# Mirrored rows by gather and scatter, one more DMA transpose, and second norms on ScalarE in a fused convolution and FFN kernel

## The chip, the cores and the metric

The kernel runs on one core of a Trainium2 chip. The metric is the device time of one execution in microseconds; lower is better. The engines are TensorE (PE), VectorE (DVE), ScalarE (ACT), GpSimd (POOL) and SyncE (SP), which here only issues DMAs.

## The reference

The input is a sequence of 2048 rows of 640 channels, in bf16. A long convolution per channel, done by FFT over 4096 points, is followed by a gated feed-forward network; both have a layer norm before them and a residual.

```python
def _A_ref(q, k, v, shift_k, ssm_k, ssm_D):        # q is the normed x
    k_shift = sum(k_pad[:, t:t + S, :] * shift_k[:, 3 - t] for t in range(4))
    kv = k_shift * v
    y = irfft(rfft(pad(kv)) * rfft(pad(ssm_k)))[:S]    # per channel, then bf16
    return q * (y + kv * ssm_D)
def _B_ref(x, w_gate, w_up, w_down):               # 640 -> 1728 -> 640
    return (silu(x @ w_gate) * (x @ w_up)) @ w_down
h  = x + _A_ref(layernorm(x), A_k, A_v, A_shift_k, A_ssm_k, A_ssm_D)
h2 = h + _B_ref(layernorm(h), B_w_gate, B_w_up, B_w_down)
```

(Cut and condensed from the original; `x` is `A_q`.)

## The kernel before

The 2048 rows are four blocks of 512, each of four tiles `q` of 128 rows. The convolution is done by block: each block of `kv` is transformed by matmuls with a fixed cosine and sine basis (`x_transform`, matrix `WX`), each segment of 512 taps of the filter likewise (`g_transform`, matrix `WG`). The spectra are multiplied and added by block pairs on DVE (`pair`, line 444, operations on 128x2560 elements), and the sums go back by `inverse` (matrix `WI`, line 598). `hbuild` joins the spectra of neighbouring segments.

The transforms use symmetry: the rows of tiles 0 and 1 of a block are needed in mirrored order. For `kv` PE mirrors them with a flip matrix (`front`, line 419; for block 0 the shift itself is made by matmuls with shifted identity matrices, `front_first`, line 394). In `inverse`, even and odd parts `es` and `os` give, by sum, tiles 2 and 3 in natural order and, by difference, tiles 1 and 0 in mirrored order. With `HOW[n] == "J"` PE flips that difference back (group `"J"`, line 618: 4 matmuls of 320 columns for each of two halves of a block), and DVE multiplies it out of PSUM (line 621).

The filter segment `p` is needed with taps on partitions. `gload` either loads it plainly and turns it with 20 matmuls of 128 columns and four ACT copies (lines 315 and 319), or, where `TRANS` names the segment, uses one DMA transpose of 640 KB issued by SP (line 304). The skip weight `ssm_D` (`drow`) is added to tap 0 of segment 0 by five one-row matmuls (line 317).

A layer norm has statistics (`ln`; on ACT lines 528 to 532, or on DVE for block 0's second norm), a power -1/2 on POOL (`root`, line 551), and a scaling (`scale`), on DVE (line 564) or ACT (lines 560 and 561). `XACT` lists the pairs (block, norm) with the scaling on ACT. Before each pow a small DVE reduction is placed, the "port op" (`port`, line 538): [...] the pow waits for it. For pairs in `XACT` a one-element DVE copy of `rstd` (line 553), called the `h` copy below, follows the pow.

The normed rows `hl` go through a DMA transpose to `hT` (line 649), and `ffn` runs gate and up projections (line 686, 512 columns), evicts them on ACT (lines 691 and 698), multiplies on DVE (line 700), and does the down projection (line 717, 320 columns). For blocks 0 to 2 the residual is added on PE (line 714) and ACT copies the result out (line 723); for block 3 DVE adds it (line 725). Output tiles use two buffers `ot`, by `m % 2`.

PSUM has four tiles: two ("A") for the convolution, two ("F") for filter transforms and FFN; a group takes one until its eviction.

The order is written out: every step is registered with `add(engine, ...)` and numbered, and `SEQUENCE` is a list of all 1017 numbers. Each engine runs its steps in that order, SP and POOL their DMA issues too, and waits where data aren't there. The list came from a planner, for which `pr`, `t0`, `lag`, `kb` and the durations are costs; they have no effect once the list is written out.

`HOW`, `BACK`: with `HOW[n] == "G"` a block's first two tiles of `x` are gathered from HBM in mirrored order (`load_x`, `mirror`, two indirect DMAs on POOL, by a table of indices `idx`), the difference needs no flip, and its residual is added mirrored; with `BACK[n] == "S"` output tiles 0 and 1 are scattered back by indirect DMAs on POOL, each after a port op that waits for the output copy.

Of the kernel before, what the change touches and what calls it, by code (L numbers as in the profile page):

```python
# [16 lines left out]
D = 640  # L17
FF = 1728
P = 128
# [74 lines left out]
ACC = ()  # L94
MOVES = ()
RES = (0, 1, 2)
XACT = [(n, 1) for n in (1, 2, 3)]
VEC = (0,)
SPAN = 96
TURN = ()  # L100
HOW = 'JJJJ'
BACK = "SSSS"
TRANS = {2: 28, 3: 28}
WARM = (0.43, 5, 0)
SEQUENCE = [int(i) for i in """
0 19 205 5 1 8 67 3 7 20 6 21 77 23 4 2 10 11 76 13 12 14 15 17 16 68 18 70 69 71 72 62 74 73 22 75 59 32 51 56 52 49 63 57 78 54 79 50 64 80 26 53 81
24 55 84 25 27 28 58 204 85 30 213 60 29 31 82 33 61 212 83 90 41 65 34 86 88 87 66 35 42 206 9 92 100 89 207 43 93 101 122 208 94 44 118 102 91 95 45
333 103 96 214 46 104 97 47 36 105 98 215 48 106 99 216 37 107 217 110 226 154 38 227 39 209 155 109 221 234 196 40 220 332 108 162 320 197 170 163
111 164 171 112 188 113 134 189 114 228 135 165 116 115 222 172 117 229 156 173 119 223 123 157 230 136 120 124 190 231 121 445 142 158 446 191 125
138 137 126 198 159 127 143 199 160 235 144 192 161 128 139 224 210 140 193 178 145 211 141 225 200 179 146 129 437 321 218 201 180 147 219 194 132  # L110
181 130 133 148 232 166 195 149 233 131 182 167 186 260 183 252 439 174 253 261 152 168 249 175 153 237 262 184 169 150 447 151 263 254 202 187 438
255 185 256 203 448 264 176 247 265 257 266 177 246 322 236 323 440 267 250 324 258 325 327 239 248 328 240 344 449 339 329 345 326 251 330 340 331
334 441 341 450 259 269 335 342 356 336 346 343 337 357 268 238 351 338 270 347 353 368 460 348 352 459 349 442 272 454 363 354 241 350 364 355 242
271 408 358 369 407 243 273 359 360 380 405 276 361 274 365 375 366 244 275 370 367 376 392 362 377 461 381 277 278 393 284 434 371 279 378 285 281
280 394 435 382 404 372 406 373 453 300 286 374 383 301 282 379 306 462 298 302 283 482 387 384 385 388 299 287 386 389 463 307 390 433 395 290 291
396 308 391 397 443 309 400 398 455 288 415 573 289 464 436 678 416 312 677 561 401 399 417 292 402 303 313 293 304 409 403 305 456 310 418 296 311
457 410 297 294 479 419 411 295 444 480 412 451 413 421 314 452 483 414 420 422 458 423 315 465 670 318 427 316 319 466 485 424 317 493 501 481 574
428 502 562 425 487 429 494 430 484 495 467 568 669 496 488 431 503 497 486 504 563 498 491 505 565 585 564 489 569 566 506 499 567 468 586 679 575
570 571 576 671 500 577 580 578 572 490 581 582 597 469 579 587 598 509 426 583 588 472 680 507 584 592 492 508 589 593 590 609 511 470 604 610 594
591 595 510 605 599 596 513 606 600 471 621 512 539 607 622 474 517 608 601 515 475 616 514 602 617 473 603 611 516 618 518 612 633 540 672 634 613  # L120
519 476 635 614 673 477 674 541 712 520 619 526 521 522 628 681 525 615 682 629 542 620 692 523 630 691 527 623 631 432 524 547 624 528 632 625 544
641 711 626 531 636 642 627 713 643 548 813 532 637 801 693 685 529 686 645 530 714 646 543 644 647 638 533 549 534 639 545 675 550 651 640 553 546
535 554 648 537 694 652 538 649 687 551 653 536 552 478 695 654 715 802 663 676 650 814 555 688 683 664 684 556 689 655 696 665 690 656 559 557 560
666 697 657 717 558 658 716 667 659 698 660 719 741 661 699 733 742 808 718 734 743 810 720 809 735 721 811 803 744 702 812 804 825 723 805 662 820
806 826 722 700 815 701 807 816 724 837 817 821 818 725 822 832 823 838 668 736 819 824 827 703 727 737 849 706 833 726 738 829 828 728 745 830 850
739 729 834 839 835 740 831 840 836 841 731 704 844 842 730 746 845 861 846 856 749 847 862 705 857 848 843 707 732 747 851 748 708 858 751 852 874
859 873 853 863 860 854 875 245 709 750 868 753 864 909 869 855 754 865 757 866 761 752 779 765 870 876 710 755 871 780 877 758 756 881 922 872 759
867 882 883 781 760 878 762 766 879 763 891 782 764 783 884 767 892 769 880 768 770 893 784 785 771 894 773 786 788 772 775 885 776 787 774 886 910
791 789 792 887 777 790 778 895 888 795 793 903 797 921 794 896 798 904 889 796 905 799 800 906 897 907 890 898 899 900 916 901 917 918 911 919 920
912 913 933 923 914 934 915 924 925 928 926 927 929 930 945 940 931 946 932 941 942 935 943 944 936 937 957 947 938 958 939 948 949 952 950 951 953  # L130
954 969 908 959 955 970 956 964 965 966 982 981 961 960 902 967 976 962 983 963 977 968 978 971 979 972 973 984 974 975 985 980 986 989 987 988 993
990 991 994 992 995 999 996 1000 997 1001 1002 1011 1003 1012 1004 998 1013 1014 1005 1015 1006 1016 1007 1008 1009 1010
""".split()]


def dve(n, psum=False):
    return (120 + n) / 960 if psum else 0.06 + n / 1920
# [7 lines left out]
def kernel(  # L145
# [123 lines left out]
    def load(q, dst, src, w, pr, kb, r=(), dur=0.45, after=(), t0=0.0):  # L269
        eng = {"SP": nc.sync, "ACT": nc.scalar, "POOL": nc.gpsimd}[q]  # L270
        before = plan.stage
        if not before and w:
            plan.stage = "load " + w[0]
        add(q, dur, lambda: eng.dma_start(out=dst, in_=src), r=r, w=w, pr=pr, kb=kb, after=after, t0=t0)
        plan.stage = before
# [25 lines left out]
    @stage  # L301
    def gload(p, pr, q="SP"):
        if p in TRANS:
            add("SP", 5.5, lambda: nc.sync.dma_start_transpose(gT[p], A_ssm_k[:, p * MB:(p + 1) * MB]), w=[f"gT{p}"], pr=pr, kb=640, t0=TRANS[p])
            return
        kc = kch[p % 2]
        load(q, kc, A_ssm_k[:, p * MB:(p + 1) * MB].rearrange("(c q) t -> q c t", q=P), [f"kch{p % 2}"], pr, 760)
        for kt in range(4):
            g = (TP[p], "T", p, kt)

            def mm(g=g, kt=kt):
                out = ps(g).rearrange("p a b -> p (a b)")
                for c in range(5):
                    dd = p == 0 and kt == 0
                    nc.tensor.matmul(out[:, c * P:(c + 1) * P], kc[:, c, kt * P:(kt + 1) * P], ident, start=True, stop=not dd)
                    if dd:
                        nc.tensor.matmul(out[:, c * P:(c + 1) * P], ident[0:1, :], drow[:, c * P:(c + 1) * P], start=False, stop=True)
            add("PE", 0.6, mm, r=["flip", f"kch{p % 2}"] + (["drow"] if p == 0 and kt == 0 else []), w=[g], pr=pr + 50, acq=(TP[p], g))
            add("ACT", act(D), lambda g=g, kt=kt: nc.scalar.copy(gT[p][:, kt, :], ps(g).rearrange("p a b -> p (a b)")[:, 0:D]),
                r=[g], w=[gTk[p]], pr=pr - 40, rel=(TP[p], g))  # L320

    def wcast(t):
        g = ("A", "w", t)
# [49 lines left out]
        return bass.AP(tensor=kk.tensor, offset=kk.offset + row * D, ap=[[D, n], [1, 4 * D]]).rearrange("p (a b) -> p a b", a=4)  # L373

    def first_loads():
        load("SP", kfirst[:], kk[0:MB, :].rearrange("(m p) d -> p m d", p=P), ["x1_0", "x1_1", "x1_2", "x1_3"], -98, 640)
        load("SP", hT[0][:].rearrange("p a b -> p (a b)").rearrange("p (a b) -> p a b", a=4), vv[0:MB, :].rearrange("(m p) d -> p m d", p=P), ["v0all"], -96, 640)
        load("SP", WG, WG_h.ap(), ["WG0", "WG1"], -95, 1024)

    @stage  # L380
# [281 lines left out]
    def ffn(n, pr):  # L662
# [38 lines left out]
        if n == 0:  # L701
            down_loads()
        plan.stage = f"down {n}"
        for m in range(4):
            gr = ("F", "D", n, m)
            back = m < 2 and HOW[n] != "J" and BACK[n] == "T"
            out_by = "S" if m < 2 and HOW[n] != "J" and BACK[n] == "S" else ""
            res = n in RES or back
            parts = [(0, 4), (4, 8), (8, 12), (12, 14)]
            for i, (c0, c1) in enumerate(parts):  # L710
                def mm(gr=gr, m=m, c0=c0, c1=c1, res=res, back=back):
                    if c0 == 0 and res:
# [6 lines left out]
                add("PE", 2 * (c1 - c0 + (i == 0 and res)) * 0.137, mm, r=[f"wd{i}"] + (["wd4", "tz", "wz"] if i == 3 else []) + [f"x{b}_{m}", (("F", "U", n, 13), 0)] + [f"tT{c}" for c in range(c0, c1)] + ([(gr, i - 1)] if i else []),  # L719
                    w=[(gr, i)], pr=pr + 20 + m, acq=("F", gr) if i == 0 else None)  # L720
            s = m % 2
            if res:
                add("ACT", act(D), lambda gr=gr, m=m, s=s: nc.scalar.copy(r3(ot[s][:]), ps(gr)[:, :, 0:NH]), r=[(gr, 3)], w=[f"o{s}"], pr=pr - 9000, rel=("F", gr))
            else:
                add("DVE", dve(D, True), lambda gr=gr, m=m, s=s: TA(r3(ot[s][:]), ps(gr)[:, :, 0:NH], r3(xin[b][:, m, :])), r=[(gr, 3), f"x{b}_{m}"], w=[f"o{s}"], pr=pr - 9000, rel=("F", gr))
# [90 lines left out]
```

## Time and profile before

| what | us |
|---|---|
| median of 3 runs | 289.55 (289.06 to 289.61) |
| profiled execution, its own time | 288.89 |
| its span, first to last instruction | 287.1 |
| PE busy | 277.1 |
| DVE busy | 220.8 |
| ACT busy | 198.4 |
| POOL busy | 18.6 |
| HBM traffic over the span | 139 GB/s |

The profile is of one execution. "Busy" of PE includes matmuls that overlap in the pipeline, so counts times the spacing of back-to-back matmuls say more than the share. The chain of waits is followed back from the last instruction, and names for each piece the engine and line that held it. A group's row reads: line, engine, operation, output and inputs, shapes, count, busy time and mean nanoseconds, then idle time before it and who ended it. In the DMA rows, "us to landing" is from issue until the data are there.

### The profile page before, as it was taken

The page shows a single profiled execution, that of the slowest core. Times are in us where ns is not written, and L with a number is a line of the kernel's source. Part 1 is how long each engine was busy: PE and PEld are TensorE (multiplying, and loading weights), DVE is VectorE, ACT ScalarE, POOL GpSimd, SP SyncE. Part 2 cuts the span into 40 slices and gives each one's busy share as a digit, 9 for nine tenths or more (in the row PEclk, how much of TensorE's full clock was granted, in tenths as well). Part 3 has the DMA queues.
Part 4 walks back from the last instruction along what each step waited for, and adds up shares of the span by engine and source line. Part 5 has one row for each costly group of instructions (what it writes and reads, how often), then busy time and mean ns, then how long its engine had stood idle before and what let it go on. Part 6 is the DMA issues. An engine that isn't in the chain of part 4 may idle for free.

```text
span 287.1 us, 4448 instructions
## 1 busy us (share of the span) xinstructions
PE 277.1 (97%) x1680; PEld 164.3 (57%) x1680; DVE 220.8 (77%) x299; ACT 198.4 (69%) x388; POOL 18.6 (6%) x22
## 2 busy tenths in 40 slices
PE   7899999999999999999999999999999989999994
PEld 2577777776444546764455467645455665444673
DVE  1738999999999999999999999999997511111222
ACT  5898755878785999367879995498958954545300
POOL 0003000010001001300004011000100110000000
PEclk9999999999999999999999999999999999999999
DMA  7999691363369847685653567456441391665011
GB/s 222 327 289 257 171 354 32 116 183 71 87 172 313 232 169 199 141 221 173 161 138 69 177 191 184 116 160 159 99 109 46 32 200 24 159 158 143 1 48 46
DMA packets 67946, 44.13 MB, mean 154 GB/s; under 512 B 25490, under 2 KB 66003, under 8 KB 67796
## 3 DMA queue, kind: packets, MB, share of 16 engines
q1 hardware_dynamic: 67778, 43.64, 56.0%
q8 instruction: 13, 0.21, 0.3%
q10 hardware_dynamic: 146, 0.20, 0.3%
q14 instruction: 9, 0.07, 0.1%
HBM read 37.28 MB, written 2.62 MB: 139 GB/s over the span
## 4 chain that ended last, share of the span: by engine, by line
DVE 54%; PE 22%; ACT 10%; DMA 7%; issue 5%; SPq 0%; DVEq 0%; ACTq 0%
DVE s L444 19%; DVE T L444 13%; PE psF L686 10%; PE psF L717 8%; DVE k L362 5%; DVE tT L700 3%; DMA hT<-in_A_v_dram 3%; PE psA L394 2%; DMA wu<-in_B_w_up_dram 2%; DMA k<-in_A_k_dram 2%; DVE k L367 2%; ACT sg L691 2%; ACT xln L561 2%; ACT junk L531 2%; ACT uc L698 2%
## 5 line engine op out<-in xcount | busy, mean ns | idle before, releaser
L686 PE MATMUL psF<-hT,wg 128*128 128x512 bf16 x280 | 68.6, 379 | 0.7 <-ACT uc L698 0.7
L686 PE MATMUL psF<-hT,wu 128*128 128x512 bf16 x260 | 63.6, 379 | 0.2 <-DMA wu<-in_B_w_up_dram 0.2
L717 PE MATMUL psF<-wd,tT 128*128 128x320 bf16 x448 | 63.3, 299 | 0.0
L717 PEld LDWEIGHTS <-tT 128*128 128x128 bf16 x448 | 43.8, 98 | 17.2
L444 DVE TENSOR_TENSOR s<-s,T 128x2560 bf16<-128x2560 bf16 x32 | 47.4, 1493 | 0.1
L444 DVE TENSOR_TENSOR T<-s,s 128x2560 bf16<-128x2560 bf16 x32 | 47.3, 1491 | 0.0
L691 ACT ACTIVATE sg<-psF 128x512 bf16<-128x512 f32 (+1 forms) x56 | 33.2, 596 | 20.2 <-DVE tT L700 12.0
L700 DVE TENSOR_TENSOR tT<-sg,uc 128x512 bf16<-128x512 bf16 (+1 forms) x56 | 23.0, 424 | 30.7 <-ACT uc L698 30.4
L686 PEld LDWEIGHTS <-wg 128*128 128x128 bf16 x280 | 27.4, 98 | 31.1 <-issue 1.2
L686 PEld LDWEIGHTS <-wu 128*128 128x128 bf16 x260 | 25.3, 98 | 30.2 <-DMA wu<-in_B_w_up_dram 0.7
L698 ACT CAST uc<-psF 128x512 bf16<-128x512 f32 (+1 forms) x56 | 32.8, 586 | 10.3 <-PE psF L686 9.8
L551 POOL TENSOR_TENSOR rstd<-var,mhalf 128x2 f32<-128x2 f32 (+2 forms) x15 | 18.1, 1207 | 213.9 <-ACT var L532 181.2
L345 PEld LDWEIGHTS <-s 128*128 128x128 bf16 x256 | 25.0, 98 | 9.7
L347 ACT CAST s<-psF 128x640 bf16<-128x640 f32 x32 | 22.1, 696 | 11.2 <-PE psF L345 11.1
L345 PE MATMUL psF<-wd,s 128*128 128x320 bf16 x192 | 28.5, 299 | 0.0
L439 ACT CAST s<-psA 128x640 bf16<-128x640 f32 x29 | 19.5, 696 | 9.4 <-PE psA L434 9.4
L531 ACT ACTIVATE junk<-x,sm 128x640 uint8<-128x640 bf16 x28 | 23.2, 830 | 0.5
L434 PE MATMUL psA<-kv,WX 128*128 128x320 bf16 x128 | 21.0, 299 | 0.0
L444 DVE TENSOR_TENSOR s<-s,s 128x2560 bf16<-128x2560 bf16 x14 | 20.8, 1487 | 0.0
L528 ACT ACTIVATE junk<-x 128x640 uint8<-128x640 bf16 x28 | 20.7, 738 | 0.0
L598 PE MATMUL psA<-s,WI 128*128 128x320 bf16 x128 | 19.0, 299 | 0.3 <-DVE s L444 0.2
L362 DVE TENSOR_TENSOR k<-k,w 128x2560 bf16<-128x2560 bf16 x12 | 17.7, 1488 | 0.0
(72 smaller groups left out, 242.9 us busy)
## 6 DMA issues: line engine op xcount, KB each, us to landing
k<-in_A_k_dram SPq DMA_DIRECT2D x12, 640.0 KB, 5.5
wu<-in_B_w_up_dram SPq DMA_DIRECT2D x24, 320.0 KB, 3.8
wg<-in_B_w_gate_dram SPq DMA_DIRECT2D x24, 320.0 KB, 3.3
x<-in_A_q_dram SPq DMA_DIRECT2D x4, 640.0 KB, 7.4
out_dram<-o SPq DMA_DIRECT2D x16, 160.0 KB, 2.1
v<-in_A_v_dram SPq DMA_DIRECT2D x12, 160.0 KB, 3.2
wd<-in_B_w_down_dram SPq DMA_DIRECT2D x3, 640.0 KB, 6.4
tT<-in_A_ssm_k_dram SPq DMA_DIRECT2D x2, 640.0 KB, 7.8
```

Of the source, the lines that this page charges most:

```text
L345: nc.tensor.matmul(ps(g)[:, h, 0:NH], WG[:, kt, ct * P:(ct + 1) * P], gT[p][:, kt, h * NH:(h + 1) * NH], start=(kt == 0), stop=(kt == 3))
L347: add("ACT", act(D), lambda g=g, ct=ct: nc.scalar.copy(r3(G[p][ct // 4][:, ct % 4, :]), ps(g)[:, :, 0:NH]), r=[g], w=[Gk[p] + "cs"[ct // 4 ...
L362: add("DVE", dve(4 * D), lambda: nc.vector.tensor_mul(kd[:], kd[:], w4[:]), r=["w4"] + ks, w=[kn], pr=pr)
L434: nc.tensor.matmul(ps(g)[:, h, 0:NH], WX[:, kt, ct * P:(ct + 1) * P], kv[:, base + kt, h * NH:(h + 1) * NH], start=(kt == 0), stop=(kt == 1))
L444: add("DVE", dve(n * D), lambda: f(o, a, b), r=ks(ak) + ks(bk), w=ks(ok), after=["WG0", "WG1"] if ok[:2] == "s7" else [], pr=pr)
L528: add("ACT", 0.74, lambda: nc.scalar.activation(junks[j][:], src, ACT.Copy, scale=-1.0 / D, accum_out=s[:, 0:1]), r=[xk], w=[k + "a", f"ju ...
L531: nc.scalar.activation(junks[j][:], src, ACT.Square, bias=s[:, 0:1], accum_out=s[:, 1:2])
L686: i = nc.tensor.matmul(ps(gr)[:, which, :], w[:, kt, cc * P:(cc + 1) * P], hT[b][:, kt, :], start=(kt == 0), stop=(kt == 4))
L691: apart(gr, 0, nc.scalar.activation(sg[s][:z, :], ps(gr)[:z, 0, :], ACT.Silu))
L698: add("ACT", act(MB), lambda gr=gr, s=s, z=z, merged=merged: nc.scalar.copy(uc[s][:z, :], ps(gr)[64:128, 0, :] if merged else ps(gr)[:, 1, ...
L700: add("DVE", dve(MB), lambda c=c, s=s, z=z: TM(tT[:z, c * MB:(c + 1) * MB], sg[s][:z, :], uc[s][:z, :]), r=[f"sg{s}", f"uc{s}"], w=[f"tT{c ...
L717: nc.tensor.matmul(ps(gr)[:, h, 0:NH], tT[:, c * MB + m * P:c * MB + (m + 1) * P], wd[:, c, h * NH:(h + 1) * NH], start=(c == 0 and not re ...
```

## The change

- `TRANS` names segment 1 too, so `gload(1)` is one DMA transpose on SP in place of a plain load, 20 matmuls and four ACT copies.
- `HOW` is `"GGJJ"`: blocks 0 and 1 gather tiles 0 and 1 of `x` mirrored (four indirect DMAs on POOL), their `inverse` has no `"J"` matmuls, and output tiles 0 and 1 of both blocks are scattered (four indirect DMAs on POOL, each with a port op before it). SP loads the index table `idx` first.
- `XACT` gains (0, 1), (1, 2) and (2, 2): four scalings of block 0's first norm and eight of the second norms of blocks 1 and 2 move from DVE to ACT; each of these roots gets an `h` copy on DVE.
- `drow` is added to tap 0 of segment 0 by one DVE operation on one partition instead of five matmuls.
- The last output tile is done half by half: 14 matmuls for columns 0 to 319, their addition and store, then the other half.
- `SEQUENCE` is new. SP now starts with `idx`, `drow`, segment 0, `k` and `v` of block 0, `WX`, the transpose of segment 1, tiles 2 and 3 of `x`, `WG`; before, it started with a `v` tile of block 1, segment 1, `k`, `v`, `x`, segment 0, `drow`, the transpose of segment 2, `WG`, `WX`. The transposes of segments 2 and 3 now follow each other after `WI`. PE turns segment 0 first, then does the shifts of tiles 2, 0, 1, 3 and then three groups of `g_transform(0)` before `x_transform(0)`; before, segment 1 came first, and the turning of segment 0 stood between shifts 3, 0, 1, 2. On POOL the gathers of block 0 come first; each gather of block 1 stands before a root; the first scatter of block 0 stands before the root of block 1's tiles 3 and 0, the second after it; both scatters of block 1 stand after block 2's last root. On ACT the new second-norm scalings stand beside the output copies of the down projections of blocks 0 and 1. The new `h` copies stand far behind their roots.

```diff
-XACT = [(n, 1) for n in (1, 2, 3)]
+XACT = [(n, 1) for n in range(4)] + [(1, 2), (2, 2)]
...
-HOW = 'JJJJ'
+HOW = 'GGJJ'
 BACK = "SSSS"
-TRANS = {2: 28, 3: 28}
+TRANS = {1: 0, 2: 0, 3: 0}
 WARM = (0.43, 5, 0)
 SEQUENCE = [int(i) for i in """
...
             def mm(g=g, kt=kt):
                 out = ps(g).rearrange("p a b -> p (a b)")
                 for c in range(5):
-                    dd = p == 0 and kt == 0
-                    nc.tensor.matmul(out[:, c * P:(c + 1) * P], kc[:, c, kt * P:(kt + 1) * P], ident, start=True, stop=not dd)
-                    if dd:
-                        nc.tensor.matmul(out[:, c * P:(c + 1) * P], ident[0:1, :], drow[:, c * P:(c + 1) * P], start=False, stop=True)
+                    nc.tensor.matmul(out[:, c * P:(c + 1) * P], kc[:, c, kt * P:(kt + 1) * P], ident, start=True, stop=True)
...
+        if p == 0:
+            add("DVE", dve(D), lambda: TA(gT[0][0:1, 0, :], gT[0][0:1, 0, :], drow), r=["drow"], w=[gTk[0]], pr=pr - 40)
...
+        def last_tile(gr, m, s):
+
+            def done(h, i):
+                if not h:
+                    apart(gr, 0, i)
+
+            for h in range(2):
+                cols = slice(h * NH, (h + 1) * NH)
+
+                def mm(h=h, cols=cols):
+                    for c in range(14):
+                        i = nc.tensor.matmul(ps(gr)[:, h, 0:NH], tT[:, c * MB + m * P:c * MB + (m + 1) * P], wd[:, c, cols], start=(c == 0), stop=(c == 13))
+                        if h:
+                            apart(gr, 1, i)
...
+                add("DVE", (120 + NH) / 960, lambda h=h, cols=cols: done(h, TA(ot[s][:, cols], ps(gr)[:, h, 0:NH], xin[b][:, m, cols])),
+                    r=[(gr, h), f"x{b}_{m}"], w=[f"o{s}h{h}"], after=[f"o{s}"], pr=pr - 9000, rel=("F", gr) if h else None)
+                load("SP", oo[n * MB + m * P:n * MB + (m + 1) * P, cols], ot[s][:, cols], [], pr - 300, 80, r=[f"o{s}h{h}"])
...
+            if (n, m) == (NB - 1, 3):
+                last_tile(gr, m, s)
+                continue
```

## The prediction

> **What bounds the kernel now.** I read the totals first, then three stretches of the span, then the chain that ended last, and then the queues at the start. Totals and stretches (columns: stretch, its length, and each engine's busy time with its instructions):
>
> ```profile
> PE 277.1 (97%) x1680; PEld 164.3 (57%) x1680; DVE 220.8 (77%) x299; ACT 198.4 (69%) x388; POOL 18.6 (6%) x22
> 0.00:21.90 21.90, 18.85 (x113) 11.21 (x114) 9.24 (x11) 16.51 (x32) 0.47 (x7) 1.00 0.94 280
> 21.90:253.00 231.10, 227.80 (x1388) 135.32 (x1385) 205.01 (x276) 172.70 (x342) 18.11 (x15) 1.00 0.58 154
> 268.30:283.60 15.30, 15.20 (x112) 10.72 (x110) 3.00 (x6) 1.17 (x2) 0.00 (x0) 1.00 0.10 33
> ```
>
> A busy PE is not a PE at its peak, so I count work. In the chain
>
> ```profile
> 253.00 15.28 PE psF L686 x70
> 268.29 15.23 PE psF L717 x112
> 283.54 0.82 DVE o L725
> ```
>
> nothing stands between matmuls: a 512-column one costs 15.28/70 = 0.218 us, a 320-column one 15.23/112 = 0.136 us. The first spectral transform of block 0 (line 345) starts at 21.90. From there to 283.5 PE has 540 of the first (117.6 us) and 1028 of the second (139.8 us): 257.4 us of work in 261.6. So only 4.2 us is lost after 21.9. PE's work bounds the kernel, with the late start and a 3.6 us tail around it. DVE, 205 of 231 us busy in the long stretch, runs close behind: it must feed PE on time.
>
> The start, as three engines show it:
>
> ```profile
> 6.60 1.25 PE L315 MATMUL psF<-perm,tT 128*128 128x128 bf16 x10
> 11.47 3.26 PE L394 MATMUL psA<-s,perm 128*128 128x320 bf16 x14
> 21.90 3.42 PE L345 MATMUL psF<-wd,s 128*128 128x320 bf16 x24
> 25.16 1.25 PE L434 MATMUL psA<-kv,WX 128*128 128x320 bf16 x8
> ...
> 6.27 7.90 SPq L304 DMA_TRANSPOSE wd<-in_A_ssm_k_dram  x1
> 14.21 0.58 SPq L274 DMA_DIRECT2D s<-const_wg  x1
> 22.46 5.43 SPq L304 DMA_TRANSPOSE hT<-in_A_ssm_k_dram  x1
> ```
>
> PE turns filter segment 1, waits for `v`, does shifts between the turns of segment 0 and reaches line 345 only at 21.90; the input transform (line 434) waits for DVE until 25.16. A transpose of 640 KB holds SP for 5.4 to 7.9 us, and what follows waits.
>
> **The change, part by part.**
>
> *PE.* Two inverses lose their J matmuls: 16 of 32 on line 618, 16 x 0.136 = -2.2 us, all in the full stretch. Twenty turning matmuls of segment 1 and five for `drow` go too, from the start, where they count only through the start time.
>
> *Start.* Segment 0 is now loaded first, then `k`, `v`, `WX`, then the transpose of segment 1. The first product waited for `k` (issued 1.66, product at 8.70). Now 640 KB lies ahead of it instead of 800, with issue some 0.4 us later: I take 8.4. Products of tiles 2, 1, 0 end at 8.4 + 3 x 1.44 = 12.7. PE: `v` still near 10.4, its turn to 11.5, tile 2's shift 3.26 to 14.8, `v`'s second turn 0.6, tile 0 to 16.4, tile 1 (14 x 0.149) to 18.4, tile 3 to 20.4. So line 345 starts near 20.3, not 21.90: -1.6 us. Tile 3's product with `v` (0.82) and the two sums (0.8 each) follow to 22.9, so line 434 starts at 22.9, 2.2 earlier; the three G groups put ahead of it (3 x 1.09) cover the gap. The new addition of `drow` (nearest row, 0.49 us) lies while DVE waits for a shift. `WG` now stands behind 2.4 MB, the transpose and half of `x`. [...] the traced transposes took 5.4 and 7.9 us for 640 KB; [...] by the trace SP is free at 12.5 and `WG` (5.7 us before) lands at 18 to 19. [...] both are ahead of 20.3, the second barely. If it is 3 us worse, the gain is gone. Bounds: +1.5 to -3. The transposes of segments 2 and 3 move to after 20 us; their users come 16 groups later (past 35), cover enough.
>
> *DVE.* Twelve scalings leave for ACT (4 for block 0's first norm, 8 for the second norms): 12 x 0.44 = -5.3. Each half of two inverses trades 0.49 + 0.49 + 0.82 + 2 x 0.49 for 2 x 0.49 + 2 x 0.82: -0.6 over four. Added: four port ops (0.25), six `h` copies (0.15), `drow`: +2.4. Net -3.5, plus 2.2 earlier: DVE leads by about what PE gains, which is what the steady stretch needs. The `h` copies stand long after their pows; a wait there is zero. The port op after each down copy makes DVE wait for ACT and PE: if that copy is late, pair products queue behind it. In the new order one or two other DVE ops lie between copy and port op, so 0, at worst 1 us each.
>
> *ACT.* -4 x 0.69, +12 x 1.2 (0.28 + 0.92) = +11.6 us. Room by stretch:
>
> ```profile
> 104.00:116.00 12.00, 11.99 (x81) 7.65 (x79) 11.95 (x19) 11.64 (x28) 2.53 (x2) 1.00 0.54 139
> 116.00:128.00 12.00, 12.00 (x87) 8.37 (x86) 11.89 (x13) 4.47 (x8) 1.50 (x1) 1.00 0.65 160
> 148.00:172.00 24.00, 23.29 (x139) 13.36 (x137) 23.82 (x37) 23.22 (x52) 3.90 (x2) 1.00 0.50 141
> 172.00:184.00 12.00, 12.00 (x88) 8.33 (x87) 11.97 (x17) 5.83 (x12) 1.20 (x1) 1.00 0.71 183
> ```
>
> ACT is full at each inverse and half empty in the down projection after it. The order puts the new scalings (4.8 us a block) in those, where 7.5 and 6.2 us are free: 0. Without that cover each would delay an eviction by 1.2 us and PE by as much. The chain root, scaling, transpose, next FFN grows by 2 x 0.75 us; counted in the two orders at 0.136 us a matmul, 11.3 us of PE work stands behind block 1's last root before FFN 1, against 8.1 before: covered.
>
> *POOL.* Four gathers and four scatters join its queue, and SP loses the same traffic. What waits: the pows behind them, ACT's norms of block 0 (for gathers) and, for scatters, the ACT copy that reuses the output buffer. Rows:
>
> ```profile
> ACT o L723 <- DMA out_dram<-o: 4.1, 2, 2.1
> L551 POOL TENSOR_TENSOR rstd<-var,mhalf 128x4 f32<-128x4 f32 x4 | 7.2, 1810 | 93.1 <-ACT var L532 93.0
> L551 POOL TENSOR_TENSOR rstd<-var,mhalf 128x1 f32<-128x1 f32 x4 | 2.2, 545 | 23.4 <-ACT var L532 23.4
> ```
>
> A small pow takes 0.55 us beside a quiet DVE and up to 2.93 beside a full one: [...] With 2.1 us from issue to landing that makes a scatter 2.1 to 4.5 us. [...] Both stay below the 8 us or more of PE work that the new order has between copy and reuse; the first wait of 2.1 on an output buffer stood in this same place and cost PE nothing. Price 0 to 2 us for all four; I take 0.5. Block 0's gathers run in the first 8 us, DVE mostly idle, landing between 8 and 14, needed at 12: 0 to +1.5, within the start's bounds.
>
> *Tail.* The last tile is done in two halves: PE's 28 matmuls stay, the last addition falls from 0.82 to an estimated 0.45 (half the columns), the last store to 80 KB: -0.4 (0 to -0.9).
>
> Sum: -2.2 - 1.6 + 0.5 - 0.4 = -3.7 on the profiled execution's 288.89 (span 287.1 and 1.8 around it). That execution lies 0.66 below the median, 289.55; I move the difference there: 285.8.
>
> **Rivals.** *DVE takes over as the bound*: PE is ahead but the pair products aren't, because the port ops and the ACT detour of `xln` eat DVE's lead. For it: DVE is full from 24 to 216 us. Against: its 3.5 us less work. Then only start, half of J and tail remain, about -2: 287.5. *The start does not come earlier* (the change doesn't do what it says there: three transposes hold SP, `WG` at 22): -2.2 - 0.4 + 0.5, 287.4; with 3 us lost, 290.5. *Slower: POOL starves.* [...] the pows queue behind, the scaling and the ACT copy wait, and PE runs out of PSUM slots. The first 8 us are free, so it decides where a scatter takes over 10 us: each beyond that is paid by ACT and PE. At 12 us, four cost 8 us: net +4, 293; at 11, no change.
>
> **How the numbers follow.** Main course 0.62 (283.5 to 287.5), DVE 0.14, late start 0.10 (0.06 faster, 0.02 the same, 0.02 slower), POOL 0.14 (0.02 the same, 0.12 slower); of DVE's 0.14, 0.01 is no change. A measurement tells about 0.2%, 0.6 us, here. Faster by more: 0.62 + 0.13 + 0.06 = 0.81; same 0.05; slower 0.14. The range, 282.6 to 290.0, takes the start's and steady stretch's better bounds below and leaves out most of the POOL case above.
>
> **What would show it.** Right: line 345 first at about 20.3 and line 434 at 22.9; line 618 x16; PE near 273 us busy; lost time after the first line 345 still near 4 us; last addition near 0.45 us. Wrong: ACT's o copies waiting over 3 us for output DMAs, pows over 3 us, DVE waits at the port ops, or PE idle waiting for `hT` at an FFN's start.

## The result, and the profile after

The changed kernel took 285.74 us (median of 4, 284.65 to 286.94), beside 289.31 us (288.63 to 289.61) for the kernel before on the same chip: ratio 0.9881 [0.9836, 0.9925]. A repeat on another chip gave 0.9915 [0.9894, 0.9937]. So the gain is 2.5 to 3.5 us; the forecast was 285.8.

The profiled execution took 285.87 us (before 288.89), span 284.1. Its totals, and stretches (stretch, length, then busy time and instructions of PE, PE's weight loads, DVE, ACT and POOL, then granted clock, DMA share and GB/s):

```profile
PE 273.3 (96%) x1639; PEld 160.8 (57%) x1639; DVE 218.3 (77%) x295; ACT 207.3 (73%) x408; POOL 37.1 (13%) x30
0.00:20.92 20.92, 16.58 (x88) 9.50 (x89) 9.54 (x12) 13.81 (x28) 4.82 (x11) 1.00 0.87 266
20.92:281.00 260.08, 256.68 (x1554) 151.26 (x1551) 208.26 (x282) 193.50 (x380) 32.28 (x20) 1.00 0.56 147
```

PE has lost 3.8 us of busy time: 41 matmuls fewer, that is 16 flips, 20 for the turning of segment 1 and five for `drow`. The start, and the end of the chain that ended last:

```profile
8.71 1.29 PE L314 MATMUL psF<-perm,tT 128*128 128x128 bf16 x10 [0.36 <-ACT wd L316]
9.12 1.49 DVE L383 TENSOR_TENSOR s<-x,w 128x2560 bf16<-128x2560 bf16 x1 [4.95 <-DMA x<-in_A_k_dram]
11.73 0.71 PE L401 MATMUL psF<-hT,perm 128*128 128x320 bf16 x2 [1.74 <-DMA hT<-in_A_v_dram]
12.24 1.27 PE L393 MATMUL psA<-s,perm 128*128 128x320 bf16 x4
13.31 1.01 PE L393 MATMUL psA<-k,perm 128*128 128x320 bf16 x3
16.03 3.15 PE L393 MATMUL psA<-k,perm 128*128 128x320 bf16 x22
19.01 2.07 PE L393 MATMUL psA<-s,perm 128*128 128x320 bf16 x14
20.92 3.42 PE L344 MATMUL psF<-wd,s 128*128 128x320 bf16 x24
...
3.89 9.31 SPq L304 DMA_TRANSPOSE wd<-in_A_ssm_k_dram  x1
13.87 0.47 SPq L274 DMA_DIRECT2D s<-const_wg  x1
...
277.16 3.82 PE psF L714 x28
```

(Line numbers up to about 700 are one lower than before.) PE waits 1.74 us for `v`, then shifts without a pause into the first spectral transform at 20.92. `WG` is no wait, though issued at 13.87. The shifts run at two rates: four matmuls between 12.24 and 13.31 are 0.267 us each, fourteen between 19.01 and 20.92 are 0.136.

One more wait shows, at the start of FFN 1, and the POOL rows have grown:

```profile
127.90 1.24 PE L685 MATMUL psF<-hT,wg 128*128 128x512 bf16 x5 [1.17 <-DMA hT<-hl]
L550 POOL TENSOR_TENSOR rstd<-var,mhalf 128x2 f32<-128x2 f32 (+2 forms) x15 | 26.0, 1732 | 177.8 <-ACT var L531 146.8 <-DVE var L510 31.0
L752 POOL DMA_INDIRECT out_dram<-o,idx x4 | 5.0, 1252 | 5.8 <-DMA out_dram<-o,idx 5.1 <-ACT o L745 0.4 <-ACT junk L530 0.2
L745 ACT CAST o<-psF 128x640 bf16<-128x640 f32 x12 | 8.3, 688 | 7.5 <-PE psF L736 7.5
```

A scatter occupies POOL for 1.25 us on the mean, and the second one of block 1 first waits 5.1 us for the first. ACT's output copies wait for PE alone; the waits of 4.1 us on output DMAs are gone.

### The profile page after: what moved, and what is told of

It reads as the page before. It is cut to its first block, busy times and chain, and to the rows that moved or that the text cites. A ratio compares the mean times of both kernels' runs of the same rounds, so it can differ in the third digit from the quotient of the medians.

```text
span 284.1 us, 4423 instructions
## 1 busy us (share of the span) xinstructions
PE 273.3 (96%) x1639; PEld 160.8 (57%) x1639; DVE 218.3 (77%) x295; ACT 207.3 (73%) x408; POOL 37.1 (13%) x30
## 4 chain that ended last, share of the span: by engine, by line
DVE 34%; PE 25%; ACT 8%; DMA 4%; issue 3%; DVEq 0%; ACTq 0%
DVE s L443 14%; PE psF L685 12%; PE psF L736 9%; DVE T L443 9%; DVE tT L699 3%; DMA hT<-hl 2%; DVE k L361 2%; DMA wu<-in_B_w_up_dram 2%; ACT junk L530 2%; PE psF L714 1%; ACT junk L527 1%; ACT sg L690 1%; ACT uc L697 1%; DVE k L366 1%; DVE k L367 1%
## 5 line engine op out<-in xcount | busy, mean ns | idle before, releaser
L736 PE MATMUL psF<-wd,tT 128*128 128x320 bf16 x420 | 60.0, 299 | 0.0
L736 PEld LDWEIGHTS <-tT 128*128 128x128 bf16 x420 | 41.1, 98 | 16.1
L550 POOL TENSOR_TENSOR rstd<-var,mhalf 128x2 f32<-128x2 f32 (+2 forms) x15 | 26.0, 1732 | 177.8 <-ACT var L531 146.8
L699 DVE TENSOR_TENSOR tT<-sg,uc 128x512 bf16<-128x512 bf16 (+1 forms) x56 | 22.9, 421 | 32.1 <-ACT uc L697 32.0
```

The costliest lines, as they stand in the source:

```text
L550: add("POOL", 0.8, lambda: nc.gpsimd.tensor_tensor(rstd[:, c0:c1], var[:, c0:c1], mhalf[:, 0:c1 - c0], op=ALU.pow), r=deps + gkey + ["mhal ...
L699: add("DVE", dve(MB), lambda c=c, s=s, z=z: TM(tT[:z, c * MB:(c + 1) * MB], sg[s][:z, :], uc[s][:z, :]), r=[f"sg{s}", f"uc{s}"], w=[f"tT{c ...
L736: nc.tensor.matmul(ps(gr)[:, h, 0:NH], tT[:, c * MB + m * P:c * MB + (m + 1) * P], wd[:, c, h * NH:(h + 1) * NH], start=(c == 0 and not re ...
```

## Experiments

I count each profiled execution as in the prediction: from PE's first spectral transform to PE's end (start plus length of its last group), less the matmuls between at 0.218 and 0.136 us (and, with segment 1 turned by PE, its twenty of 128 columns at 0.055). What is left is lost.

| kernel | first transform | PE's end | between | matmuls | lost |
|---|---|---|---|---|---|
| before | 21.90 | 283.50 | 261.6 | 257.4 | 4.2 |
| before, tail only | 23.31 | 284.90 | 261.6 | 257.4 | 4.2 |
| before, PE kept busy | 21.10 | 282.85 | 261.8 | 257.4 | 4.4 |
| changed | 20.92 | 280.97 | 260.1 | 255.2 | 4.9 |
| changed, repeat | 21.95 | 280.44 | 258.5 | 255.2 | 3.3 |
| segment 1 turned by PE | 22.25 | 284.33 | 262.1 | 256.3 | 5.8 |
| changed, plain stores | 22.16 | 281.58 | 259.4 | 255.2 | 4.2 |
| block 1 flipped by PE | 22.01 | 284.29 | 262.3 | 256.3 | 6.0 |
| the same, later in PE's order | 22.17 | 282.92 | 260.8 | 256.3 | 4.5 |
| second norms back on DVE | 22.08 | 284.18 | 262.1 | 255.2 | 6.9 |
| changed, PE kept busy | 20.48 | 279.10 | 258.6 | 255.2 | 3.4 |
| and `WG` first | 19.12 | 279.78 | 260.7 | 255.2 | 5.5 |
| and `hT` first | 20.19 | 282.89 | 262.7 | 255.2 | 7.5 |
| and `k` later | 19.74 | 279.98 | 260.2 | 255.2 | 5.0 |

**The changed kernel again** (unchanged).

> The changed kernel once more, so that the variants of this series have it on the same chip. Expected 3.6 us below the kernel before (3.0 to 4.2), as measured. First line 344 near 20.9 us, PE idle once for about 1.2 us before FFN 1.

286.00 us (285.34 to 287.19), ratio 0.9915 [0.9894, 0.9937]: 2.5 us by the ratio, below the 3.0 to 4.2 that I expected, though the intervals of the two measurements overlap. The first transform came at 21.95, a microsecond later than in the first profile, and there was no wait at FFN 1; PE still ended half a microsecond earlier:

```profile
11.83 0.71 PE L401 MATMUL psF<-hT,perm 128*128 128x320 bf16 x2 [1.84 <-DMA hT<-in_A_v_dram]
16.61 3.60 PE L393 MATMUL psA<-k,perm 128*128 128x320 bf16 x22
21.95 3.42 PE L344 MATMUL psF<-wd,s 128*128 128x320 bf16 x24
```

`v` was turned 0.1 us later than in the first profile; the rest of the microsecond is the slow rate, which lasted until 17.5 here and until 15.5 there. A single profile thus tells the start no better than within a microsecond or more.

**Block 1 flipped by PE.**

```diff
-HOW = 'GGJJ'
+HOW = 'GJJJ'
...
-                add("PE", 2 * 0.137, mm, r=["flip", f"kv{q}"], w=[g], pr=pr, acq=("A", g), after=["rev"] + [("A", "J", n - 1, 1)])
+                add("PE", 2 * 0.137, mm, r=["flip", f"kv{q}"], w=[g], pr=pr, acq=("A", g), after=["rev"])
```

> Block 1 back to the flip on PE: 8 more matmuls on line 617, no gather and no scatter for block 1, its output stored by SP. The order is else that of the changed kernel. Theory (PE's work bounds): slower than the changed kernel by 8 x 0.136 = 1.1 us, that is 2.5 us below the kernel before. Rival (POOL's gathers, scatters and port ops cost about what the matmuls did): same as the changed kernel or faster, 3.6 to 5 us below before.

289.32 us, ratio 1.0014 [0.9997, 1.0031]: 2.9 us (by the ratios) to 3.3 above the repeat, where the theory had 1.1. Its waits of PE (engine, line and what it waited for, total, times, longest):

```profile
PE psA L617 <- ACT es L601: 1.2, 1, 1.2
PE psA L418 <- DVE y L620: 1.0, 1, 1.0
```

Both stand where I had put the matmuls back, too close behind the evictions. So the run mixes 1.1 us of work with 2.2 us of waits of its own order and could not decide. I repeated it with both groups later:

**Block 1 flipped by PE, later in the order.** As above; the first group behind the next gate and up projection, the second inside the first down tile.

> The same as the run with block 1's flip matmuls put back, but they stand later in PE's order (the first group after the projections that followed it, the second inside the first down tile), so that PE does not wait for the evictions or hold a PSUM slot: block 1 has plain loads and stores, 8 flip matmuls (1.09 us) and DVE's products out of PSUM. Theory: the extra cost of 3.3 us seen with the early placement was 2.1 us of PE waits of my placement; here it is +1.1 to +1.8 us against the changed kernel, about 287.3. Rival: DVE's and ACT's lead is what block 1's gathers bought, and the cost stays at 3 us or more wherever the matmuls stand (289 or above).

288.54 us, ratio 0.9985 [0.9970, 1.0000]: 2.0 us (by the ratios) to 2.5 us above the repeat, more than the theory's 1.1 to 1.8 and less than the rival's 3. The row that carries the difference:

```profile
PE psF L685 <- ACT uc L697: 2.1, 3, 1.6
...
103.28 0.92 ACT L560 ACTIVATE xln<-x,sm,rstd 128x640 bf16<-128x640 bf16 x1 [0.90 <-DVE y L620]
```

ACT waits for DVE's product out of PE's flip, since the next half's `xln` uses the same buffer, and PE then waits 1.6 us for an eviction behind it. Matmuls (1.1) and this wait (1.6) make 2.7, the difference of the two spans (286.3 and 283.6), in one profile of each. In this order a flip on PE costs its matmuls and one more hand-over from PE through DVE to ACT; how much of the second a better order would hide stays open. In the profile before, PE waits about 0.5 us in all at its 32 flip matmuls.

**Second norms of blocks 1 and 2 back on DVE.**

```diff
-XACT = [(n, 1) for n in range(4)] + [(1, 2), (2, 2)]
+XACT = [(n, 1) for n in range(4)]
```

> Only the 8 second-norm scalings of blocks 1 and 2 go back from ScalarE to VectorE, at the same places of the order, and their h copies go: DVE +8 x 0.44 - 4 x 0.15 = 2.9 us more, ACT 8 x 1.2 = 9.6 us less. Theory (PE bounds, DVE has a lead of that size): 0 to 1 us slower than the changed kernel. Rival (DVE is the bound): 2.9 us slower, so only 0.7 us below the kernel before. Second rival (ACT's detour is what delays hT and FFN 1): faster than the changed kernel by up to 1.2 us.

288.56 us, ratio 0.9987 [0.9970, 1.0004]: 2.1 to 2.6 us above the repeat for 2.9 us more DVE work (8 scalings of 0.44, less four `h` copies of 0.15). My "0 to 1 us" fell and the rival nearly held. The place:

```profile
177.97 0.45 DVE L563 TENSOR_SCALAR hl<-x,sm,rstd 128x640 bf16<-128x640 bf16 x1 [0.60 <-DMA hT<-hl]
179.85 0.83 DVE L421 TENSOR_TENSOR kv<-kv,rev 128x1280 bf16<-128x1280 bf16 x1
180.71 0.83 DVE L422 TENSOR_TENSOR kv<-kv,rev 128x1280 bf16<-128x1280 bf16 x1
181.60 1.26 PE L433 MATMUL psA<-kv,WX 128*128 128x320 bf16 x8 [1.56 <-DVE kv L422]
```

A scaling of block 2 stands ahead of the sums that make block 3's `kv`, waits 0.60 us for its buffer, and PE waits 1.56 us for the sums. That is nearly half of the 3.6 us more between first transform and end; the rest lies in smaller waits. The scalings stand at the places that the new order gave to ACT. How much of the 2.1 to 2.6 us is DVE's work as such, and how much this order, no run separates.

**Segment 1 turned by PE.**

```diff
-TRANS = {1: 0, 2: 0, 3: 0}
+TRANS = {2: 0, 3: 0}
```

> Segment 1 loaded plainly at the place where its DMA transpose stood, and turned by 20 matmuls and four ACT copies between the first transforms. Theory (start set by the landing of k and v and by the shifts; PE's work counts): [...] ACT +2.8 in a busy stretch, so 1.2 to 2 us slower than the changed kernel, first line 344 within 0.5 us of 20.9. Rival (the 9.3 us for which SP is held set the start): first line 344 at least 1 us earlier and the time the same or better.

288.67 us, ratio 0.9988 [0.9973, 1.0003]: 2.1 to 2.7 us above the repeat. The first transform came at 22.25, not within 0.5 us of 20.9 as I had said, but within 0.3 of the repeat, though `WG` was issued at 7.22 instead of 13.97. So no gain shows from freeing SP of the DMA transpose; the rival fell. Twenty matmuls (about 1.1 us of PE) and waits of PE on ACT between 24 and 32 us (1.2 us) account for about what was lost. These waits too belong to the places where I put the matmuls.

**The tail alone**, in the kernel before: `last_tile` and nothing else of the change.

> The kernel before with nothing changed but the last output tile, done half by half (14 matmuls, addition and store, then the other half). My step for the tail said -0.4 us, and the changed kernel's profile has a last addition of 0.49 us and a tail 0.45 us shorter. If the steps add up, this kernel is 0.4 to 0.5 us below the kernel before, ratio about 0.9985. Rival: the first half's addition and store get in the way of the second half's matmuls or of the second store, and nothing is left (0 +- 0.2).

288.41 us beside 289.06, ratio 0.9981 [0.9969, 0.9992], -0.55 us by the ratio: the step adds up. Its profile also showed what the start of the kernel before can be:

```profile
11.77 3.94 PE L394 MATMUL psA<-s,perm 128*128 128x320 bf16 x14
23.31 3.42 PE L345 MATMUL psF<-wd,s 128*128 128x320 bf16 x24
```

Here fourteen shifts took 3.94 us and the first transform came at 23.31; in the profile before they took 3.26 and it came at 21.90, with the same instructions.

**PE kept busy in the changed kernel.** Four matmuls of 512 columns on zeros fill its wait for `v`:

```diff
-WARM = (0.43, 5, 0)
+WARM = (0.43, 5, 4)
...
-        g = ("F", name)
+        t = "A" if r else "F"
+        g = (t, name)
```

> The changed kernel with four more 512-column matmuls on memory set to zero, put between the turning of segment 0 and the turn of v, where PE waits 1.7 us (their result is never used; a one-element DVE copy frees their PSUM). Theory: the start is set by the rate of PE, because after that wait the shifts ran at 0.267 us for 320 columns until about 16 us and at 0.136 us after it. With the wait filled, the shifts run at 0.136 us from 12 us on and the first spectral transform (line 344) starts at 19.7 to 20.2 instead of 20.9 and 21.95; all of that reaches the end: -0.8 to -1.5 us against the changed kernel. Rival 1: DVE's products and v's landing set the start, the shifts wait for them, and line 344 stays at 20.9 or later: 0. Rival 2: the start comes earlier but DVE, full from 24 to 216 us, gives it back at the first inverse: line 344 near 20, time unchanged within 0.3.

284.05 us, ratio 0.9835 [0.9812, 0.9858], 1.3 to 2.3 us below the changed kernel's two results, for the 0.8 to 1.5 of the theory: the shifts ran fast and the time fell.

```profile
9.87 1.45 PE L289 MATMUL psA<-hl 128*128 128x512 bf16 x4
12.19 0.45 PE L402 MATMUL psF<-hT,perm 128*128 128x320 bf16 x2 [0.86 <-DMA hT<-in_A_v_dram]
12.47 0.71 PE L394 MATMUL psA<-s,perm 128*128 128x320 bf16 x4
17.63 2.06 PE L394 MATMUL psA<-s,perm 128*128 128x320 bf16 x14
...
PE psF L345 <- DMA s<-const_wg: 0.8, 1, 0.8
```

`v` came half a microsecond later than in the changed kernel's profile, yet every shift ran at 0.136 us (four from 12.47 to 13.01) and they ended near 19.7. Then PE waited 0.8 us for `WG`, until 20.48, outside my 19.7 to 20.2: the wait that I had called barely covered appears once the shifts are fast.

**Plain stores in place of the scatters.**

```diff
-            out_by = "S" if m < 2 and HOW[n] != "J" and BACK[n] == "S" else ""
+            out_by = ""
```

> The changed kernel with the four scatters of output tiles 0 and 1 of blocks 0 and 1 replaced by plain stores on SP at the same places in the order, and without the four port ops before them (so these tiles leave with their rows mirrored within a tile and swapped between the two: only the row order of the output differs). Theory (my step: the POOL traffic costs 0.5 us, 0 to 2): 0 to 0.6 us below the changed kernel, most of it DVE's four port ops (1.0 us of DVE work). Rival 1, POOL starves: the pows of block 1 and of blocks 2 and 3 come much earlier, and the time falls by 1.5 us or more. Rival 2: four more stores in SP's queue hold the transposes of the norms and loads up, and the kernel is slower by 0.3 to 1 us.

286.21 us, ratio 0.9895 [0.9876, 0.9915], overlapping the repeat's interval. By the ratios four scatters and four port ops cost 0.6 us together, by the medians nothing; the intervals would allow 1.4. The gathers are still in this run. The pows stay as they were without any scatter on POOL:

```profile
L550 POOL TENSOR_TENSOR rstd<-var,mhalf 128x2 f32<-128x2 f32 (+2 forms) x15 | 24.5, 1634 | 190.9 <-ACT var L531 159.1 <-DVE var L510 31.8
```

So it isn't the scatters that make them long, and the rival "POOL starves" fell for the scatters.

**PE kept busy in the kernel before**, with three such matmuls.

> The kernel before with three more 512-column matmuls on memory set to zero between the turning of segment 1 and the turn of v (result unused), where its PE waits 1.05 us. In the profile before and in that of the tail-only kernel the first spectral transform (line 345) starts at 21.90 and at 23.31 with an unchanged start: the two differ in how long the shifts ran at 0.267 us a matmul. Theory: this slow rate costs the kernel before as much as the changed one, and the change's own gain at the start is the rest. Then line 345 starts near 20.5 here, the time falls by 1 to 2 us to about 287.5, and the distance to the changed kernel with the same addition (284.05) stays at 3 to 3.7 us. Rival: the changed kernel is the only one slowed, since the kernel before has shorter gaps; then this kernel stays within 0.4 us of the kernel before.

288.05 us beside 288.91, ratio 0.9971 [0.9960, 0.9982]: -0.84 us, less than the 1 to 2 of the theory, more than the rival's 0.4. The first transform came at 21.10, not 20.5: nearly all shifts are fast here (fourteen in 2.22 us, before 3.26), and that is all the fill can give to this start. With the slow rate taken out of both, the changed kernel is 3.9 to 4.0 us faster (284.05 and 288.05, on two chips), above the 3 to 3.7 that I expected; 0.6 of it is the start (20.48 and 21.10).

**PE kept busy, and `WG` first.** SP's order is now `idx`, segment 0, `k`, `v`, `WX`, `drow`, `WG`, `x`, and then the transpose of segment 1.

> The changed kernel with the four extra matmuls in PE's wait, and SP's first issues in another order: drow behind WX, then WG and x's tiles 2 and 3, and only then the transpose of segment 1 (before: drow second, transpose, x, WG). With PE kept busy alone, v was turned at 12.19 and line 344 waited 0.78 us for WG until 20.48. Theory: loads start 0.45 us earlier, so v is turned near 11.75 and WG is there; line 344 starts at 19.2 to 19.5, about 1.1 us earlier, and the time is 283.0 to 283.4. Rival 1: WG's 1 MB now shares the DMA engines with v and k, v lands later (12.5 or more), line 344 comes at 20 or after, no gain. Rival 2: segment 1's transpose, issued later and behind x, is late for the filter transforms of segment 1 or holds up the loads behind it on SP, and the time rises.

283.40 us (282.85 to 284.96), ratio 0.9800 [0.9775, 0.9824]: the fastest of the study, 0.65 us below PE kept busy alone by the medians, with overlapping intervals. The start is as expected:

```profile
11.50 0.73 PE L402 MATMUL psF<-hT,perm 128*128 128x320 bf16 x2
19.12 3.42 PE L345 MATMUL psF<-wd,s 128*128 128x320 bf16 x24
...
PE psF L686 <- DMA hT<-hl: 1.0, 1, 1.0
PE psA L434 <- DVE s L439: 0.8, 1, 0.8
```

This execution (284.67 us, above the median) gives the whole of its earlier start back: it loses 5.5 us after it, where PE kept busy alone lost 3.4, and 1.8 of that is in these two waits.

**And `hT` first**: two SP loads (`wg` for FFN 1 and `k` for block 3) moved behind the transposes of block 1's normed rows.

> As the run with WG first, and two SP loads for later work (320 KB of wg for FFN 1's second chunk, 640 KB of k for block 3) moved from between the DMA transposes of block 1's normed rows to behind them. In the changed kernel's profile PE waited 1.17 us for the last of these (issued 121.47, landed 6.18 us later), in its repeat not at all. Theory: these loads ahead are what made that transpose slow, the wait at FFN 1's start appears where PE is early, and an earlier start makes it bite; then this kernel has no wait for hT at FFN 1 and is 0 to 1 us faster than the one with WG first. Rival: the wait is set by ACT's second-norm scalings and not by the DMA, and nothing changes; or wg then comes late and PE waits for it instead (slower).

287.23 us, ratio 0.9931 [0.9904, 0.9957]: 3.8 us slower than without the move. No wait for `hT` is left, but its rival came in a worse form:

```profile
129.50 1.56 PE L686 MATMUL psF<-hT,wu 128*128 128x512 bf16 x5 [2.05 <-DMA wu<-in_B_w_up_dram]
130.85 2.34 PE L686 MATMUL psF<-hT,wg 128*128 128x512 bf16 x5
...
130.00:134.00 4.00, 4.00 (x12) 1.46 (x11) 1.83 (x2) 1.18 (x2) 0.00 (x0) 0.57 0.58 182
```

PE waits 2.05 us for `wu`; then the granted clock is 0.57 for 4 us, and 12 matmuls fill what 18 would have at 0.218 us each.

**And `k` later**: as the run with `WG` first, only `k` moved, behind four weight loads.

> As the run with WG first (not the one after it), with one load moved: the 640 KB of k for block 3, issued between the DMA transposes of block 1's normed rows, goes behind FFN 1's first four weight loads; the 320 KB of wg stays ahead. In the profiles where PE waited for hT at FFN 1 (1.17, 0.94 and 1.00 us) this load had been issued 2 us before the last transposes; moving wg and k together behind them removed that wait but made wu late (2.05 us) and let the granted clock fall to 0.58 for 4 us. Theory: k alone is bytes that nobody needs for 20 us, so without it both hT and wu are there in time: no wait over 0.3 us at FFN 1, and the time is 0 to 1 us below the run with WG first (283.40), 282.5 to 283.3. Rival: the weight loads themselves (wg ahead, wu behind) crowd the transposes, and the wait of about 1 us stays: 283.4 again; or x for block 2, now behind k, comes late and costs statistics (over 284).

283.98 us (282.53 to 285.54), ratio 0.9819 [0.9787, 0.9852]. The wait at FFN 1 is gone (0.2 us on `wu` is left), and the time is that of the run with `WG` first within the intervals, not below it as I had expected. As the profiles of the repeat and of PE kept busy had no such wait with `k` in its old place, that `k` causes it is not shown. Removing it is worth nothing that these runs can tell.

## Why the prediction was right

**PE's work: right.** Sixteen flip matmuls are left, PE is busy 273.3 us (forecast 273), and from first transform to end the changed kernel needs 260.1 and 258.5 us in two profiles, before 261.6 in two: a mean of -2.3 for the -2.2 of the sum. The two profiles differ by 1.6 themselves; with the four runs that change only the start, the stores or `k` (258.6, 259.4, 260.7, 260.2) the mean is 259.6, beside 261.7 of the three profiles with the old order: -2.1. The loss between is 3.3 and 4.9 us (forecast 4.2 + 0.5).

**The start: direction right, the landing of `v` wrong.** I said 20.3 for the first transform (-1.6). It came at 20.92, 21.95 and, in four other kernels with this start, between 22.01 and 22.17, a mean of 21.9; before at 21.90 and 23.31. The gain is 0.6 to 1.0 (0.7 by the means, 1.0 by the first two profiles, 0.6 with PE kept busy in both). The term that failed is "`v` still near 10.4". In the kernel before it was so:

```profile
10.44 1.25 PE L402 MATMUL psF<-hT,perm 128*128 128x320 bf16 x4 [1.05 <-DMA hT<-in_A_v_dram]
```

In these six profiles `v` was turned between 11.73 and 12.13. In the first of them it was issued 0.4 us later (2.61, before 2.22) and took 9.1 us to land (before 8.2). `k` took 7.0 us (before 6.9), although 160 KB less lay ahead of it, and its product came at 9.12 instead of 8.4. Why the loads were no faster is not shown: over the first 11.7 us the DMA engines moved 257 GB/s, before 281.

The way from there was right: I had 9.9 us from the turn of `v` to the first transform, and it took 9.2 in the first profile and 10.0 to 10.3 in the others. But I had not seen what it is made of. My shift times came from the profile before, where PE ran slow for part of them; of these 9 to 10 us, 14 to 22 matmuls at 0.267 instead of 0.136 us make 1.8 to 2.9. That this rate costs, and that it reaches the end, is shown by the run with PE kept busy (1.3 to 2.3 us). With `v` turned at 11.50 instead of 12.19 and `WG` in time, the run with `WG` first came to its first transform 1.4 us earlier, though its time fell by only 0.65 with overlapping intervals.

The order inside the start had an error of its own: I put line 434 at 22.9 and three groups of 1.09 us ahead of it, which from 20.3 makes 23.6. It came at 24.18, straight behind them and with no wait for DVE.

`WG` was the price I doubted most. I had SP free at 12.5; the transpose held it for 9.31 us, until 13.20, longer than the 5.4 and 7.9 of the profile before. `WG` came before PE needed it, but only because the shifts were slow: with fast ones PE waited 0.78 us for it.

**DVE: the sum right, its weight underrated.** DVE is busy 2.5 us less. Its operations overlap in the record: their lengths, added one by one, make 237.4 us and not 218.3, and this sum fell by 4.2 (forecast -3.5). I used this only as an argument against the rival "DVE takes over". The run with the norms back on DVE says that it counted for more: in this order 2.9 us of DVE work cost 2.1 to 2.6, about as much as PE's flips are worth. So the rival was close. That PE's 2.2 us could be collected because DVE was relieved as well fits this run, but is not separated from the order.

**ACT: right.** Its busy time grew by 8.9 us, the lengths of its operations, added one by one, by 12 (forecast +11.6); no new wait of PE came of it.

**POOL: no more than a bound, and a sign that was none.** I took 0.5 us for gathers and scatters. The four scatters and their port ops measured between nothing and 0.6; the gathers were not tested alone. Scatters took 1.25 us to issue and 3.2 us (median) to land, inside my 2.1 to 4.5; the longest took 5.4, beyond it. "Pows over 3 us" I had named as a sign of being wrong. Such rows appeared; the longest in the changed kernel, with its port op, is

```profile
70.29 6.56 POOL L550 TENSOR_TENSOR rstd<-var,mhalf 128x4 f32<-128x4 f32 x1 [10.27 <-ACT var L531]
75.90 0.24 DVE L537 TENSOR_REDUCE idle<-junk 128x1 f32<-128x96 uint8 x1
```

The record begins 5.6 us before the port op and ends 0.7 us after the end of it; the longest pow of the kernel before (2.93 us from 151.41) also ended 0.7 us after its port op. The 2.93 that I had laid to a full DVE is that one, and the 0.55 beside it is a pow of a single column without a port op. Of these two long records 5.6 and 2.0 us lie before the port op begins, and they don't show that the new traffic starved POOL: without scatters, and with neither gather nor scatter in block 1 (block 1 flipped by PE), the longer one has 6.55 us too. Two other pows of the changed kernel, 1.92 us from 114.95 and 2.40 from 146.48, had their port ops behind them by 114.16 and 146.58; why they are long is not shown.

**Tail: right**, -0.55 us alone (-0.2 to -0.9 by the interval) for the -0.4 of the sum; the last addition is 0.49 us.

**FFN 1's start: "covered" was wrong in some executions.** PE waited 1.17, 0.94 and 1.00 us for `hT` in three profiles and not in others. I had followed root, scaling and transpose, but not the 640 KB of `k` that SP issues between the transposes. Whether that load is the cause stays open; the wait costs nothing measurable, as the last run shows.

Sum as measured: -2.1 to -2.3 (POOL's price included), -0.6 to -1.0 and -0.5, together -3.2 to -3.8, against 2.5 to 3.5 found. The forecast's -3.7 had 0.6 to 1.0 too much at the start. That its 285.8 met the first median within 0.1 us is luck: the repeat gave 286.00, and 289.55, from which I subtracted, was 289.04 there. Nor do the parts add up the other way: block 1's flips, the second norms and segment 1, each put back alone, cost 2.0 to 2.7 us, together about twice the whole gain. These runs show that each piece matters in this order, not what it is worth.

## To carry to other kernels

Count the bound engine's work between its first and last real instruction: the rest splits into a start, a loss and a tail, and each part of a change can be held against one of them. Where two engines are both nearly full, ask whether relief of one is collected only with relief of the other, and test it: here 2.9 us of DVE work put back cost 2.1 to 2.6. When a piece of old work is put back for a test, look where it waits; an order made for the new form can cost more than the piece (here 2.2 us of waits with 1.1 us of flips).

## What the hardware showed that I had not expected

PE's first shifts ran at 0.267 us for 320 columns and later at 0.136. In the kernels without matmuls added in PE's wait for `v` the change came 3.5 to 6 us after the turn of `v`, at a moment that differs between executions of one kernel: near 15.5 and 17.5 us in the changed kernel and its repeat. With such matmuls it differs too: with the same instructions up to there and `v` turned at 11.50 in each, the last three kernels reached the first transform at 19.12, 20.19 and 19.74. What sets the moment is not shown.

The granted clock of the profile's rows reads 1.00 throughout this start, but the trace holds no clock record ahead of the change: its first record, full clock, begins at 15.52 in the changed kernel and at 13.90 before, and the matmul spacing changes across it (starts at 15.18, 15.44, 15.62 and 15.75; before, at 13.61, 13.87, 14.03 and 14.16). After the wait of 2.05 us at FFN 1 the rows do show a lower clock (0.57 from 130 to 134). In these starts the matmul spacing is the surer sign.

A DMA transpose of 640 KB held SP for 9.31 us with loads under way. In the changed kernel PE had no wait for `WG`, issued behind it at 13.87; with fast shifts it waited 0.8 us. The two scatters of block 1 run one after the other: the second waited 5.1 us on POOL until the first had landed.
